# The low halves of W_in, made by GpSimd and VectorE instead of TensorE

## Chip, core and metric

The kernel runs on one core of a Trainium2 chip. The metric is the device time of one execution in microseconds (us). The reference computes in fp32; the kernel keeps each fp32 operand as two fp16 numbers, a high and a low half, and multiplies with three fp16 products.

## What is computed

Causal attention with a decay (4 sequences of 576 tokens, 8 heads of 64), then two MLPs on the 2304 tokens of width 512:

```python
scores = scale * q @ k.T + cum[:, :, :, None] - cum[:, :, None, :]   # causal
x = softmax(scores) @ v                      # 2304 x 512
h = x @ w_in                                 # 512 x 2048
x2 = (h * np.tanh(softplus(h))) @ w_out      # 2048 x 512
h2 = x2 @ w2_in                              # 512 x 1024
solu = h2 * softmax(h2)
out = layer_norm(solu, g_ln) @ w2_out        # 1024 x 512
```

## The kernel before

Three stages overlap. Attention goes over the sequences b and over query tiles i of 128 tokens, in slots of 4, 2 or 1 heads: scores (L436 to L439) into PSUM, a maximum nm on VectorE (L478), the exponential p on ScalarE (L480), a rounding of p and a difference ph (L519, on GpSimd, as fp16 high and low), a transposing DMA pT on SyncE's queue (L524), and the product pv (L550 to L552). A tile ends with x (L565), its split xh (the low half on GpSimd, L569) and a transposing DMA xT, which is the input of the first MLP.

The first MLP works on blocks of 256 tokens. `up` (L787) makes 128 columns of h with 12 matmuls, four chunks of the contraction by three products; `mish` turns h into the pair gt on ScalarE, VectorE and GpSimd (its low half at L814); `down` (L831) adds the second layer. Of block 0 it walks through the 16 column groups n = 0 to 15 while the weights are still being prepared. The second MLP (Stage2) starts when attention is done.

The weights W_in and W_out come as 64-bit numbers, in 16 loads of 1 MB (8 slots each, `Weight.load`, L121, two buffers). `conv` rebuilds fp32 with three VectorE instructions (L134, L136, L138) and then forms a gram matrix with eight matmuls (L157) for a bound. Two slots make a group: `bound` turns the gram into a power-of-two scale, `high` rounds the scaled slot to fp16 on ScalarE (L199), and `low` makes the low half on TensorE, for each of the two 512-column parts of a slot a product of the fp32 weights with a scaled diagonal (L206, seen in the trace as two fp32 passes) and a product of the high half with the identity (L207), whose sum in PSUM ScalarE writes out (L208). Group g of W_in serves n = 4g to 4g+3 of `up`. In the SBUF tile win or wout the fp32 numbers of a slot lie where the next slot's halves will be, so a slot's high half is written after the previous slot's low half has been read.

These steps lie in a list, `wsteps`, in the order of the slots, W_in's pair, then W_out's pair; a step is a load, a conversion, a high or a low. The attention slots ahead of block 0 take WS0 steps each, the half-steps of the main loop WS1 each, and `up` and `down` pull further steps when theirs are missing. A scheduler then reorders each engine's instructions by its own timeline; on the chip each engine runs its list in order, waiting where a semaphore tells it to, and so does SyncE with its DMA issues. Names in the trace: wi_r and wo_r are the loaded numbers, wi_b and wo_b the bounds, wi_d and wo_d the diagonals, sp the PSUM banks that scores and low halves share.

Of the kernel before, what the change touches and what calls it, by code (L numbers as in the profile page):

```python
# [24 lines left out]
NF1 = DFF // P  # L25
# [10 lines left out]
PTB = 2  # L36
R0 = 9
GRP = [4, 2, 1, 1, 1]
WS0 = 4
WS1 = 5  # L40
WPF = 2
S2P = 1
EB = 190
DL = 2
A0 = 16
XB = 3
S2A = 10
# [30 lines left out]
def part_of(w, n):  # L78

    fr, c = divmod(2 * n, w.shape[0] // P)  # L80
    return w[c * P:(c + 2) * P, fr * 512:(fr + 1) * 512].rearrange("(s p) e -> p s e", p=P)
# [143 lines left out]
def emit(tc, q, k, v, f, w_in, w_out, w2_in, w2_out, g_ln, out):  # L225
# [6 lines left out]
    ident = const.tile([P, P], BF16, name="ident")  # L232
# [321 lines left out]
    def fin(b, i):  # L554
# [41 lines left out]
    W1 = Weight(  # L596
        tc, wst, "wi", win, NC1 * DFF // 512, lambda n: part_of(w_in, n), across, group=4,
        after=lambda: pend.get("pt"), gram=grams)
# [13 lines left out]
    def w1_split(n):  # L612
        g, r = divmod(n, W1.group)
        if r == 0:
            W1.bound(g)
            nc.vector.tensor_copy(wps[g], W1.p(g))
        W1.high(n, ident)

    def w2_split(n):
        g, r = divmod(n, W2.group)  # L620
# [1 line left out]
            W2.bound(g)  # L622
            nc.vector.tensor_tensor(rho[:, g:g + 1], wps[g], W2.p(g), op=ALU.mult)
        W2.high(n, ident)

    def w1_low(n):
        W1.low(n, ident, bank)

    def w2_low(n):
        W2.low(n, ident, bank)  # L630
# [43 lines left out]
    def slot_mid():  # L674
        n = pos["k"] - 1
        if 0 <= n < len(seq):
            step_h(*seq[n])
# [26 lines left out]
    wsteps, wdone = [], set()  # L704
    order = [(w, 2 * g + n) for g in range(4) for w in (W1, W2) for n in range(2)]
    for x in range(len(order) + WPF):
        if WPF <= x < len(order):
            wsteps.append((order[x][0].load, order[x][1]))
        if x >= WPF:
            w, n = order[x - WPF]  # L710
            wsteps.append((w.conv, n))
            if n % 2:
                for m in (n - 1, n):
                    wsteps += [(x, m) for x in ((w1_split, w1_low) if w is W1 else (w2_split, w2_low))]
    wsteps.append((w2_final, 0))

    def wgo(n):
        for _ in range(n):
            if wsteps:
                f, a = wsteps.pop(0)  # L720
                f(a)
                wdone.add((f, a))
# [32 lines left out]
    for n in range(n0 + LAG):  # L755
        slot()
        if n:
            wgo(WS0)
    raw0.close()
# [132 lines left out]
    def att_slots(n):  # L892
# [5 lines left out]
        if j == 0:  # L898
            lo = max(lo, n0 + LAG + min(need[1] - n0, (r + 1) * (need[1] - n0) // A0))
        hi = need[j + XB] - 1 if j + XB < NBLK else len(seq) + LAG  # L900
# [7 lines left out]
    for hn in range(2 * (NF + 5)):  # L908
        n, half = divmod(hn, 2)
# [4 lines left out]
        if half == 0:  # L914
            if n % 2 == 0 and 0 <= n // 2 - 1 < NF // 2:
                mish_b(n // 2 - 1)
            if att_now:
                slot_mid()
            if live:
                while n < NF1 and (w1_low, n // 4 * 2 + 1) not in wdone:  # L920
                    wgo(1)
                up(n)
        else:
            if live and n % 2:
                while n > NF1 and wsteps:
                    wgo(1)
                mish_a(n // 2)
            if n % 2 == 0 and 0 <= n // 2 - 1 < NF // 2:
                mish_c(n // 2 - 1)
            if att_now:  # L930
                slot_mid()
            tgt = n - 2 if (n > DL + 8 or n >= NF) else n - DL
            while done["d"] < min(tgt, NF):
                if done["d"] // 2 not in gts:
                    break
                while done["d"] < NF1 and (w2_low, done["d"] // 2) not in wdone:
                    wgo(1)
                down(done["d"])
                done["d"] += 1
        if att_now:  # L940
            slot_pe()
        wgo(WS1)
        while live and pos["k"] < att_slots(hn):
# [178 lines left out]
```

## Time and profile before

| | us |
|---|---|
| median of 3 runs | 863.57 (863.52 to 867.65) |
| profiled execution | 868.76 |
| its span | 867.0 |
| TensorE busy | 766.6 |
| VectorE, ScalarE, GpSimd busy | 594.2, 563.7, 394.2 |

The span is the time from the first to the last instruction of one execution that the hardware profiler recorded. An engine's busy time is the sum of its instructions' durations; matmuls are pipelined, so a busy TensorE need not be at its peak. A view of waits names who waited for whom; the chain of waits follows back, from the last instruction, what released each step.

### The profile page before, as it was taken

Reading aid. Unit: us, or ns where it says so; the run is one execution under the profiler, and the core shown is the slowest. Engines: PE = TensorE matmul, PEld = TensorE weight load, DVE = VectorE, ACT = ScalarE, POOL = GpSimd, SP = SyncE. Lnnn points to the kernel's source line nnn. Section 1 sums busy time; section 2 is a strip of 40 time slices with the busy share of each in tenths; the row PEclk is TensorE's granted clock in tenths of the full one; section 3 lists DMA queues with packets and bytes.
Section 4 is the critical chain, followed back from the end, with each engine's and each line's share of the span. In section 5 each row is a group of like instructions: output and inputs, shape, how many; then the busy total and the mean of one; then the engine's idle time right before and its main releaser. Section 6 shows DMA issues by size and latency. Waiting matters only on the chain.

```text
span 867.0 us, 16642 instructions
## 1 busy us (share of the span) xinstructions
PE 766.6 (88%) x6255; PEld 481.0 (55%) x6255; DVE 594.2 (69%) x1160; ACT 563.7 (65%) x1234; POOL 394.2 (45%) x321
## 2 busy tenths in 40 slices
PE   0468998779999997998889899987999999999998
PEld 0335565557667665676556667654555554444443
DVE  6797954668867898669887654689656454666451
ACT  5648687868878877787876666776965544333331
POOL 2232333447876565765678653226733132012110
PEclk9979999969999999999999999998999999999999
DMA  9998544487799968998797542751022424344443
GB/s 242 228 268 251 175 122 80 87 163 144 151 197 172 163 131 149 169 181 148 164 165 121 113 80 56 191 210 61 26 37 61 97 50 73 86 109 99 107 87 85
DMA packets 328573, 114.90 MB, mean 133 GB/s; under 512 B 317676, under 2 KB 317676, under 8 KB 328492
## 3 DMA queue, kind: packets, MB, share of 16 engines
q1 hardware_dynamic: 328492, 113.84, 63.7%
q8 instruction: 49, 0.80, 0.4%
q14 instruction: 32, 0.26, 0.1%
HBM read 46.59 MB, written 9.55 MB: 65 GB/s over the span
## 4 chain that ended last, share of the span: by engine, by line
PE 40%; DVE 19%; DMA 16%; ACT 9%; issue 9%; POOL 6%; SPq 1%; DVEq 0%; POOLq 0%; ACTq 0%
PE h L1030 10%; PE o L1070 10%; PE x L831 7%; PE h L787 7%; DMA pT<-ph 5%; POOL ph L519 3%; DMA wo_r<-in_moe_w_out_dram 2%; DVE ta L804 2%; POOL gt L814 2%; ACT p L480 2%; DMA xT<-xh 1%; DMA w2i_r<-in_moe_w_in_dram 1%; DVE th L808 1%; DVE vt L215 1%; DVE ph L516 1%
## 5 line engine op out<-in xcount | busy, mean ns | idle before, releaser
L831 PE MATMUL x<-wout,gt 128*128 128x512 f16 x864 | 218.4, 386 | 17.0 <-DVE x2h L860 8.4
L787 PE MATMUL h<-xT,win 128*128 128x256 f16 x1728 | 221.0, 279 | 1.8 <-DMA xT<-xh 1.8
L519 POOL TENSOR_TENSOR ph<-p,ph 128x512 f16<-128x512 f32 (+4 forms) x120 | 155.4, 1301 | 92.0 <-ACT ph L518 42.3
L787 PEld LDWEIGHTS <-win 128*128 128x128 f16 x1728 | 170.0, 100 | 45.1 <-issue 5.5
L814 POOL TENSOR_TENSOR gt<-th,gt 128x512 f16<-128x512 f32 x72 | 92.5, 1286 | 128.7 <-ACT gt L813 122.0
L831 PEld LDWEIGHTS <-gt 128*128 128x128 f16 x864 | 80.5, 99 | 96.4 <-issue 12.5
L1058 POOL TENSOR_TENSOR z<-sl,z 128x1024 f16<-128x1024 f32 x18 | 38.7, 2150 | 138.2 <-DVE s2c L1037 111.3
L1030 PE MATMUL h<-w,x2T 128*128 128x512 f16 x432 | 98.0, 379 | 0.9 <-POOL w L222 0.9
L1070 PE MATMUL o<-wo,zT 128*128 128x512 f16 x432 | 96.5, 379 | 0.5 <-DMA zT<-z 0.5
L550 PE MATMUL pv<-vt,pT 128*128 128x64 f16 (+3 forms) x480 | 68.6, 200 | 23.3 <-DMA pT<-ph 22.9
L808 DVE SCALAR_TENSOR_TENSOR th<-ta,th 128x512 f32<-128x512 f32 x72 | 64.6, 898 | 30.5 <-ACT ta L807 28.0
L436 PE MATMUL sp<-kt,qa 128*128 128x128 f16 (+3 forms) x480 | 68.7, 219 | 15.6 <-ACT p L480 9.6
L480 ACT ACTIVATE p<-sp,nm 64x64 f32<-64x64 f32 (+7 forms) x128 | 61.2, 484 | 27.3 <-DVE nm L478 12.9
L813 ACT CAST gt<-th 128x512 f16<-128x512 f32 x72 | 44.4, 616 | 44.2 <-DVE th L808 42.7
L437 PE MATMUL sp<-kt,qb 67*128 67x128 f16 (+3 forms) x480 | 70.5, 219 | 2.5 <-DMA kt<-dd 2.5
L1030 PEld LDWEIGHTS <-x2T 128*128 128x128 f16 x432 | 42.3, 98 | 51.4 <-issue 1.2
L1070 PEld LDWEIGHTS <-zT 128*128 128x128 f16 x432 | 42.2, 98 | 51.5 <-DMA zT<-z 0.9
L804 DVE TENSOR_SCALAR ta<-ta 128x512 f32<-128x512 f32 x72 | 53.7, 746 | 23.5 <-ACT ta L799 23.2
L550 PEld LDWEIGHTS <-pT 128*128 128x128 f16 (+3 forms) x480 | 44.3, 100 | 45.8 <-DMA pT<-ph 29.6
L552 PE MATMUL pv<-vt,pT 128*128 128x64 f16 (+3 forms) x480 | 67.8, 195 | 0.0
L551 PE MATMUL pv<-vt,pT 128*128 128x64 f16 (+3 forms) x480 | 67.8, 195 | 0.0
L805 ACT ACTIVATE ta<-ta 128x512 f32<-128x512 f32 x72 | 45.3, 631 | 34.0 <-DVE ta L804 33.8
(231 smaller groups left out, 1462.6 us busy)
## 6 DMA issues: line engine op xcount, KB each, us to landing
wi_r<-in_moe_w_in_dram SPq DMA_DIRECT2D x8, 1024.0 KB
wo_r<-in_moe_w_out_dram SPq DMA_DIRECT2D x8, 1024.0 KB
rawk<-in_k_dram SPq DMA_DIRECT2D x25, 256.0 KB
rawv<-in_v_dram SPq DMA_DIRECT2D x25, 256.0 KB
x2d<-x2h SPq DMA_DIRECT2D x18, 256.0 KB
out_dram<-ro SPq DMA_DIRECT2D x18, 256.0 KB
w2i_r<-in_moe_w_in_dram SPq DMA_DIRECT2D x4, 1024.0 KB
w2o_r<-in_moe_w_out_dram SPq DMA_DIRECT2D x4, 1024.0 KB
```

Source lines behind the costliest of these rows:

```text
L436: nc.tensor.matmul(o, qa[:, h, r0:r1_], kc[:, h, a0:a1], start=True, stop=False)
L437: nc.tensor.matmul(o, qb_[:67, h, r0:r1_], kc[:67, H + h, a0:a1], start=False, stop=(c != i))
L480: nc.scalar.activation(pv[:m, g * (i + 1) * P + off:g * (i + 1) * P + end], s3[:, g, off:end], AF.Exp, bias=nm[:m, g:g + 1], accum_out=rs[ ...
L519: nc.gpsimd.tensor_tensor(p4[:, :, 1], pv3, p4[:, :, 0], op=ALU.subtract)
L550: nc.tensor.matmul(o, pT[a0:a1, k, :m], vh, start=(c == 0), stop=False)
L787: nc.tensor.matmul(ph, win[:, (fi // 4) * NC1 + c, col:col + P], x[:, lx * NC1 + c, :], start=(m == 0), stop=(m == 3 * NC1 - 1))
L804: nc.vector.tensor_scalar(ta, ta, E20, 1.0, op0=ALU.min, op1=ALU.add)
L808: nc.vector.scalar_tensor_tensor(th, ta, 2.5, th, op0=ALU.subtract, op1=ALU.mult)
L814: nc.gpsimd.tensor_tensor(gt[:, 1], th, gt[:, 0], op=ALU.subtract)
L831: nc.tensor.matmul(o, gt[:, lg, n % 2, t * P:(t + 1) * P], wout[:, fi, lw * 512:(lw + 1) * 512], start=(first and m == 0), stop=(last and ...
L1030: nc.tensor.matmul(h[:, half * 512:(half + 1) * 512], x[:, lx * NC1 + c, :], self.w2[:, half * NC1 + c, lw * 512:(lw + 1) * 512], start=(n ...
L1070: nc.tensor.matmul(o, zT[:, lz * NF2 + c, :], self.wo[:, c, lw * 512:(lw + 1) * 512], start=(n == 0), stop=(n == 3 * NF2 - 1))
```

## The change

For W_in the pair `high` and `low` is replaced by `split`, a function that the kernel already uses elsewhere; W_out keeps TensorE. A string W1P says, slot by slot, which form: slots 0 and 1 take the form 0 (ScalarE rounds, VectorE makes the difference), slots 2 to 7 the form 1 (ScalarE scales the fp32 numbers in place, GpSimd rounds them and makes the difference). With a step less for each slot of W_in, WS0 goes from 4 to 3 and WS1 from 5 to 4, so the steps of both weights are spread over the slots differently. The changed kernel's lines are numbered one higher up to the functions, and two lower behind them.

```diff
-WS0 = 4
-WS1 = 5
+WS0 = 3
+WS1 = 4
+W1P = "00111111"
...
     def w1_split(n):
...
-        W1.high(n, ident)
+        W1.split(n, on_pool=int(W1P[n % len(W1P)]))
...
-    def w1_low(n):
-        W1.low(n, ident, bank)
...
-                    wsteps += [(x, m) for x in ((w1_split, w1_low) if w is W1 else (w2_split, w2_low))]
+                    wsteps += [(x, m) for x in ((w1_split,) if w is W1 else (w2_split, w2_low))]
...
-                while n < NF1 and (w1_low, n // 4 * 2 + 1) not in wdone:
+                while n < NF1 and (w1_split, n // 4 * 2 + 1) not in wdone:
```

```python
def split(nc, hi, lo, x, scale, on_pool):
    if on_pool == 0:
        nc.scalar.activation(hi, x, AF.Copy, scale=scale)
        nc.vector.scalar_tensor_tensor(lo, x, scale, hi, op0=ALU.mult, op1=ALU.subtract)
        return
    nc.scalar.activation(x, x, AF.Copy, scale=scale)
    if on_pool == 1:
        nc.gpsimd.tensor_scalar(hi, x, 1.0, 0.0, op0=ALU.mult, op1=ALU.add)
...
    nc.gpsimd.tensor_tensor(lo, x, hi, op=ALU.subtract)
```

TensorE's order just ahead of the first L787, before (win is W_in's tile; the eight gram products and then L787 follow):

```order
L352 MATMUL sum<-wo_b,ones 128x1
L206 MATMUL sp_148<-win,wi_d_567 128x512
L207 LDWEIGHTS ident
L207 MATMUL sp_148<-win,ident 128x512
L206 MATMUL sp_146<-win,wi_d_567 128x512
L207 LDWEIGHTS ident
L207 MATMUL sp_146<-win,ident 128x512
L157 LDWEIGHTS win
L157 MATMUL gram<-win 128x128
```

The same place now (eight gram products of wout and then the first layer, now L785, follow):

```order
L553 MATMUL pv_1_502<-vt_1_289,pT_1_6_541 128x64
L158 LDWEIGHTS win
L158 MATMUL gram<-win 128x128
...
L207 MATMUL sp_148<-wout,wo_d_473 128x512
L207 MATMUL sp_146<-wout,wo_d_473 128x512
L208 LDWEIGHTS ident
L208 MATMUL sp_148<-wout,ident 128x512
L208 LDWEIGHTS ident
L208 MATMUL sp_146<-wout,ident 128x512
L353 LDWEIGHTS ones
L353 MATMUL sum<-wi_b,ones 128x1
```

W_in's products are gone, and of W_out one slot's stand here, behind the second tile's last pv.

VectorE's order around the maximum of the second tile's last two heads (nm_1_6, rows 75 to 85 of its list), before:

```order
L136 SCALAR_TENSOR_TENSOR win<-wi_r_361,win 128x1024
L172 TENSOR_REDUCE wo_b<-gram 128x1
L478 TENSOR_REDUCE nm_1_4_503<-sp_146 128x2
L138 SCALAR_TENSOR_TENSOR win<-wi_r_361,win 128x1024
L174 TENSOR_SCALAR wo_b<-sum 128x1
L94 TENSOR_SCALAR wo_b<-wo_b 128x1
L96 TENSOR_SCALAR wo_b<-wo_b 128x1
L134 TENSOR_SCALAR win<-wi_r_407 128x1024
L176 RECIPROCAL wo_b<-wo_b 128x1
L623 TENSOR_TENSOR rho<-wpt,wo_b 128x1
L478 TENSOR_REDUCE nm_1_6_570<-sp_146 128x2
```

Now (rows 70 to 79; L216 is the new difference of W_in, L135 to L139 are the conversions):

```order
L566 TENSOR_TENSOR x_0_0_458<-pv_0_371,rr_0_455 128x512
L139 SCALAR_TENSOR_TENSOR wout<-wo_r_303,wout 128x1024
L216 SCALAR_TENSOR_TENSOR win<-win,wi_b 128x2x512
L135 TENSOR_SCALAR win<-wi_r_349 128x1024
L569 CAST xh_0_460<-x_0_0_458 128x512
L426 COPY qb_126<-qa_2_437 64x1024
L479 TENSOR_REDUCE nm_1_6_534<-sp_147 128x2
L173 TENSOR_REDUCE wo_b<-gram 128x1
L137 SCALAR_TENSOR_TENSOR win<-wi_r_349,win 128x1024
L216 SCALAR_TENSOR_TENSOR win<-win,wi_b 128x2x512
```

The maximum stands ahead of most of that conversion and of the next one's start, and behind one difference; that of heads 4 and 5 has moved up to row 45.

GpSimd's order around the last group of W_in (rows 48 to 57 of its list), now; in the kernel before no instruction of win stands on GpSimd:

```order
L520 TENSOR_TENSOR ph_2_6_939<-p_1_129,ph_2_6_939 128x3x128
L520 TENSOR_TENSOR ph_3_0_1070<-p_0_128,ph_3_0_1070 128x4x128
L220 TENSOR_SCALAR win<-win 128x2x512
L570 TENSOR_TENSOR xh_2_1178<-x_0_2_1176,xh_2_1178 128x512
L223 TENSOR_TENSOR win<-win 128x2x512
L520 TENSOR_TENSOR ph_3_0_1070<-p_1_129,ph_3_0_1070 128x4x128
L220 TENSOR_SCALAR win<-win 128x2x512
L812 TENSOR_TENSOR gt_1680<-th_1652,gt_1680 128x512
L223 TENSOR_TENSOR win<-win 128x2x512
L812 TENSOR_TENSOR gt_1733<-th_1704,gt_1733 128x512
```

The four instructions of the group stand between xh, ph and gt; those of the two groups before it stand in a row, with one xh and one ph among the first of the last.

## Rows read from the trace of the kernel before

**Rows 1.** The page's head: busy us (share) xinstructions by engine.

```profile
span 867.0 us, 16642 instructions
PE 766.6 (88%) x6255; PEld 481.0 (55%) x6255; DVE 594.2 (69%) x1160; ACT 563.7 (65%) x1234; POOL 394.2 (45%) x321
```

**Rows 2.** Busy time by stretch: stretch, length, engines, clock, DMA share, GB/s.

```profile
36.00:78.00 42.00, 28.29 (x207) 16.00 (x207) 38.20 (x76) 27.25 (x57) 15.06 (x11) 0.88 1.00 254
78.00:156.00 78.00, 71.73 (x530) 45.36 (x529) 47.55 (x99) 60.64 (x116) 25.06 (x17) 0.98 0.51 136
156.00:190.00 34.00, 23.17 (x282) 17.70 (x281) 24.69 (x60) 24.34 (x61) 17.12 (x14) 0.76 0.70 131
190.00:867.00 677.00, 636.02 (x5182) 395.96 (x5179) 458.34 (x883) 431.37 (x954) 327.66 (x264) 0.98 0.61 119
```

**Rows 3.** Chain of waits, 45 to 140 us: start us, us, what.

```profile
61.32 3.44 PE sp L206 x4
...
68.95 0.03 PE pv L550
...
77.81 2.23 PE h L787 x19
...
80.99 0.47 PE gram L157 x8
...
129.68 4.79 POOL ph L519
...
134.49 3.71 DMA pT<-ph
```

**Rows 4.** Timeline of VectorE, 38 to 140 us: start, us, instruction.

```profile
52.71 0.67 DVE L478 TENSOR_REDUCE nm<-sp 128x2 f32<-128x512 f32 x1
...
57.04 0.68 DVE L478 TENSOR_REDUCE nm<-sp 128x2 f32<-128x512 f32 x1
```

**Rows 5.** Timeline of SyncE's queue, 0 to 160 us.

```profile
61.87 1.23 SPq L524 DMA_TRANSPOSE pT<-ph  x1
```

**Rows 6.** Timeline of TensorE, 16 to 160 us.

```profile
70.55 1.07 PE L206 MATMUL sp<-win,wi_d 128*128 128x512 f32 x2
...
71.67 1.02 PE L206 MATMUL sp<-win,wi_d 128*128 128x512 f32 x2
...
124.33 2.78 PE L787 MATMUL h<-xT,win 128*128 128x256 f16 x24
```

**Rows 7.** Groups by line, 0 to 160 us: busy, mean ns | idle before.

```profile
L206 PE MATMUL sp<-win,wi_d 128*128 128x512 f32 x32 | 18.3, 671 | 2.9 <-DVE wi_d L197 1.8 <-ACT win L208 1.1
...
L208 ACT ACTIVATE win<-sp 128x512 f16<-128x512 f32 x16 | 9.1, 592 | 4.6 <-PE sp L352 2.7 <-PE sp L207 1.9
```

**Rows 8.** Tile w, Stage2's split: ns min/median/max, first and last start.

```profile
L217 ACT ACTIVATE w<-w,w2i_b x4: 1132/1133/1134, 588.0 to 591.1; 128x1024 f32<-128x1024 f32 x4
L219 POOL TENSOR_SCALAR w<-w x4: 1046/1156/1495, 589.2 to 606.8; 128x1024 f16<-128x1024 f32 x4
L222 POOL TENSOR_TENSOR w<-w x4: 2129/2578/3100, 590.4 to 608.1; 128x1024 f16<-128x1024 f32 x4
```

**Rows 9.** Tile vt (attention's v): VectorE's difference.

```profile
L215 DVE SCALAR_TENSOR_TENSOR vt<-rawv,scv,vt x14: 734/750/1697, 44.0 to 445.7; 128x512 f16<-128x512 f32 x10, 64x512 f16<-64x512 f32 x4
```

**Rows 10.** Timeline of GpSimd, 30 to 200 us.

```profile
111.44 0.92 POOL L519 TENSOR_TENSOR ph<-p,ph 128x384 f16<-128x384 f32 x1 [8.17 <-issue]
...
128.35 6.11 POOL L519 TENSOR_TENSOR ph<-p,ph 128x384 f16<-128x384 f32 x2
```

**Rows 11.** Timeline of VectorE beside the last of these.

```profile
129.80 1.21 DVE L138 SCALAR_TENSOR_TENSOR wout<-wo_r,wout 128x1024 int32<-128x1024 int32 x1
...
132.47 1.21 DVE L138 SCALAR_TENSOR_TENSOR wout<-wo_r,wout 128x1024 int32<-128x1024 int32 x1
```

**Rows 12.** Waits of SyncE's queue, 0 to 200 us: us, times, longest.

```profile
SPq L524 <- POOL gt L814: 31.3, 2, 22.5
```

**Rows 13.** Waits of TensorE, 78 to 190 us.

```profile
PE pv L550 <- DMA pT<-ph: 9.1, 6, 2.2
```

## Prediction

> **What bounds the kernel now.** I read the page's head first: TensorE is busy for 766.6 of 867.0 us and the next engine, VectorE, for 594.2 [rows 1]. Then the busy time by stretch, since the change touches only the first 156 us [rows 2]. From 36 to 78 us VectorE is busy for 38.2 of 42 and TensorE for 28.3: the weight conversions, the preparation of the first attention rows and the scores all pass through VectorE, so it is the first limit there. From 78 us (the first matmul of the MLP's first layer, L787) to 156 us TensorE is busy for 71.7 of 78, with VectorE at 47.6 and GpSimd at 25.1: TensorE is the bound. From 156 to 190 us TensorE falls to 23.2 of 34 at a granted clock of 0.76 (part of the stretch at 1.2 GHz); it waits for the transposes of the probabilities, 9.1 us in 78 to 190 [rows 13]. From 190 us on it is busy for 636 of 677. So an early saving should reach the end, if no wait replaces it.
>
> Third, the chain of waits ahead of the first L787 [rows 3]: four fp32 passes of L206 for W_out (two low halves, 3.44 us), the attention product pv at 68.95, then VectorE, GpSimd and a transposing DMA, and L787 at 77.81. Low halves on TensorE stand on this chain.
>
> **What the change removes.** Each of the 8 slots of W_in has two low halves, each an fp32 product with the scaled diagonal (L206) and a product with the identity (L207). The trace counts fp32 passes: 32 rows are 16 products [rows 7]. From the start of one half to the next takes 1.12 us (70.55 to 71.67, [rows 6]), so TensorE loses 16 x 1.12 = 17.9 us. ScalarE loses 16 evacuations, 9.1 us [rows 7]. Its 8 roundings become 8 passes of about the same length (six fp32 scalings at 1.13, [rows 8], two roundings), so its net is -9.1; it has slack in 78 to 156 (60.6 of 78, [rows 2]) and I cost this at nothing.
>
> **What it adds.** Slots 0 and 1: two VectorE differences of 128x1024. The trace has 128x512 at 0.75 median [rows 9], so 1.5 each is my estimate, bounded by 0.75 and the 1.7 that the longest 128x512 took. Slots 2 to 7: on GpSimd a cast and a difference each. Stage 2 does the same operation on the same shape: cast 1.05 to 1.50, difference 2.13 to 3.10, medians 1.16 and 2.58 [rows 8]. That is 19 to 28 us of GpSimd, which has 53 free in 78 to 156. Throughput is no problem; latency and order are.
>
> **Term 1, the first L787 comes earlier: -7.0.** Two parts. First, the maximum (nm) of the last two heads of the second attention tile: the order has it at VectorE's row 85 in the kernel before, behind the next pair of conversions, and at row 76 now, about where heads 4 and 5 stood. These two stand at 52.71 and 57.04 [rows 4], 4.3 apart; one new difference of W_in comes ahead of it, of whose 1.5 I charge half: -3.6. Second, that tile's last transpose is issued at 61.87 [rows 5]; a transpose took 3.71 to land [rows 3], so pv could go at 65.6 and went at 68.95, behind the low halves of W_out. The order now puts these behind pv: -3.4. If only the second part arrives, the term is -3.4; with no charge for the difference it is -7.7; and if the transposes land as late as now, it is nothing.
>
> **Term 2, TensorE's work after the first L787: -5.8.** By the order, 8 low halves of W_in and 4 of W_out stand ahead of the first L787 before, and 0 and 2 now. Behind it were 8 + 12, and are 14: six fewer, 6.7 us. Two more gram groups of eight move behind it, at 0.47 each [rows 3], +0.9. The other 11.2 us of the 17.9 lay ahead of it, where TensorE was not the limit; what they are worth is in term 1.
>
> **Term 3, new waits of TensorE: +8.2.** The first-layer matmuls of columns 4, 8 and 12 (n of the function up) read slots 2 and 3, 4 and 5, 6 and 7. A pair now takes one scaling (1.13, the second is hidden) and two casts and differences in line on GpSimd: 1.13 + 2 x (1.05 + 2.13) = 7.5 us at the fastest rows, 8.6 at the medians, 10.3 at the slowest [rows 8]. Before, TensorE made these halves itself and was not idle. What covers the wait is what the order places between the reduction of the group's bound and its first matmul; for the last group 24 first-layer matmuls (2.78, [rows 6]), three fp32 products (a row shows 1.07 each, the overlap taken off 2.6 in all, [rows 6]) and, as my estimate, 1.4 of scores and pv: 6.8 us. So 0.7, 1.8 or 3.5 us stay uncovered per pair; I take the median's 1.8, three times, 5.4. In the last group the order puts xh, ph and gt between the split instructions on GpSimd, three at 0.92 [rows 10]: 2.8. Sum 8.2; ends 0 (the scheduler finds other work) and 3 x 3.5 + 2.8 = 13.3 without holds. Queued behind the splits on GpSimd are ph, whose transpose feeds pv, and the first gt, which feeds the second layer. On SyncE the load of slot 5 stands behind a transpose of such a ph. I price these in the rival below, not here.
>
> **The sum** is -7.0 - 5.8 + 8.2 = -4.6 us. The profiled execution took 868.76 (span 867.0, 1.8 around it), 5.2 above the median of the runs shown, 863.57; its sum would give 864.2. I apply the difference to the median: **859.0**.
>
> **Rival A, everything is covered: 850.8.** TensorE always has other work, term 3 is nothing, -12.8. For it: GpSimd is two thirds idle in 78 to 156 [rows 2]. Against: GpSimd's order is fixed, and a pair's latency alone exceeds the cover I found.
>
> **Rival B, GpSimd is starved by VectorE: 870.7, slower.** Between 128.35 and 134.46 us two GpSimd differences of 128x384 took 6.11 us, while one alone took 0.92 [rows 10]; one of them took 4.79 of the chain [rows 3]. In the same time VectorE ran conversions back to back, among them those at 129.80 and 132.47, each reading two tensors of the chip's memory [rows 11]. A difference held like this costs 4.79 - 0.92 = 3.9 us more. The splits of slots 2 to 5 stand, by the order, among the last conversions. With three such holds on the path the sum is -4.6 + 11.7 = +7.1. It is slower by over 0.5% from 8.9 us of holds on, between two and three. SyncE makes it worse: it already waited 31.3 us in two transposes for GpSimd [rows 12], and loads stand behind them. Against: half of the splits may fall into VectorE's gaps. The Trainium skill's page "SBUF — State Buffer", section "Who interferes with whom", says that VectorE and GpSimd share a pair of ports under an exclusive lock, and that a VectorE instruction with two inputs in SBUF and a GpSimd instruction that reads SBUF block each other for a whole instruction. By that rule every split that meets a conversion is held, and this rival would be the forecast; the 6.11 us agrees with it, the stage-2 rows of 2.13 show that it need not happen.
>
> **Rival C, the start does not move: 866.0.** The 16 DMA engines are full in 36 to 78 us (share 1.00, [rows 2]); if transposes and loads set the first L787, term 1 is nothing, and -5.8 + 8.2 = +2.4, within 0.5%. For it: the loads of the weights keep their pace. Against: from 61.32 on the chain runs through L206, pv and what follows it, not through a load of weights [rows 3].
>
> **How the numbers follow.** The bound for a difference is 0.5%, 4.3 us, about what a measurement of this kernel can tell from no change. Forecast 0.40 (855 to 863, of it 0.24 below 859.25 and 0.16 within), A 0.20, B 0.23 (0.21 slower, 0.02 within), C 0.15, and 0.02 for something slower that I don't name. Faster 0.44, same 0.33, slower 0.23. The whole program is scheduled anew behind the weights, with 41 us of TensorE's idle time in 190 to 867 to move; I allow 2 us either way for it. The range reaches from a little below A to B: 849.0 to 871.0.
>
> **What would show it.** Right: L206 with 32 rows instead of 64; the first L787 near 70 to 71 us; pv of the second tile ahead of L206; TensorE's idle time ahead of L787 put down to GpSimd's win differences, some 5 to 8 us in all; ScalarE's busy time 9 us down, GpSimd's 19 to 28 up. A: no wait of L787 on GpSimd. B: single GpSimd differences of win over 4 us beside VectorE's conversions, the last W_out load later than now relative to the first L787, the second block's first L787 not earlier than now. C: the first L787 still near 77. The prediction is wrong in its base if the stretch behind 156 us, where the transposes set the pace, swallows or adds more than 3 us by itself.

## Result and profile after

The changed kernel took **870.32 us** in the median (865.47 to 874.85, 17 runs), the kernel before 865.10 in the same comparison (861.74 to 871.09, 17 runs). The ratio is 1.0057 with a 95% interval of 1.0035 to 1.0079: slower by 5.2 us. The forecast was 4.6 us faster. The two profiled executions that are compared below lie closer together, 871.24 and 868.76, since that of the kernel before is 3.7 above its median. The time lies inside the forecast's range, beside the number of its rival B.

The page's head for the kernel after, to be laid beside [rows 1] (engine, busy us, share, instructions):

```profile
span 869.4 us, 16537 instructions
PE 755.3 (87%) x6207; PEld 477.1 (55%) x6207; DVE 599.9 (69%) x1158; ACT 555.0 (64%) x1218; POOL 419.7 (48%) x333
```

The work did move: TensorE is busy for 11.3 us less, ScalarE for 8.7 less, GpSimd for 25.5 more, VectorE for 5.7 more. But 17.9 us were taken off TensorE and only 11.3 are gone, and its idle time (span less busy) rose from 100.4 to 114.1. So the span's +2.4 is -17.9 of work removed (the forecast's 1.12 for each of 16 low halves), +6.6 of the same work done more slowly, and +13.7 of idle time. The table of stretches says where, beside [rows 2] (stretch, length, busy us of TensorE, its weight loads, VectorE, ScalarE, GpSimd, then granted clock, DMA share, GB/s):

```profile
36.00:78.00 42.00, 20.20 (x174) 14.39 (x174) 32.75 (x66) 23.13 (x50) 20.59 (x11) 1.00 0.92 239
78.00:156.00 78.00, 60.08 (x442) 37.73 (x439) 60.44 (x98) 48.90 (x91) 41.65 (x28) 0.85 0.52 141
156.00:190.00 34.00, 25.50 (x311) 17.78 (x308) 23.73 (x50) 25.67 (x62) 15.61 (x13) 0.94 0.49 96
190.00:867.00 677.00, 639.73 (x5214) 399.15 (x5211) 457.03 (x901) 437.11 (x968) 332.58 (x266) 0.98 0.61 121
```

From 78 to 156 us TensorE was idle for 6.3 us and is now idle for 17.9, and its granted clock there fell from 0.98 to 0.85: part of that stretch runs at 1.2 in place of 2.4 GHz, behind the new gaps. From 89 to 92 us, behind the idle 4.7 us ahead of L158 below, the granted clock is 0.50, and a pass of L207 takes 1.06 us there, 0.59 at 95.6. VectorE's busy time rose by 12.9 us in this stretch, though it has one instruction less there (98, before 99).

The price of the clock can be read from work that the change left alone, W_out's 32 fp32 passes, ahead of 200 us. The first line is of before (L206), the second of after (L207, the same code; busy us, mean ns | idle before):

```profile
L206 PE MATMUL sp<-wout,wo_d 128*128 128x512 f32 x32 | 17.6, 655 | 1.6 <-ACT wout L208 1.6
...
L207 PE MATMUL sp<-wout,wo_d 128*128 128x512 f32 x32 | 22.3, 820 | 5.0 <-DVE wo_d L198 2.7 <-DVE ipwo L635 2.3
```

These passes alone take 4.7 us more, most of the 6.6.

What TensorE waits for in 78 to 190 us is not what I forecast. Its waits in the kernel after (engine, line, waited for: us, times, longest), beside [rows 13]:

```profile
PE pv L551 <- DMA pT<-ph: 9.2, 5, 4.0
PE gram L158 <- DVE win L139: 4.7, 1, 4.7
PE sp L207 <- DVE wo_d L198: 2.5, 1, 2.5
PE sp L207 <- DVE ipwo L635: 2.3, 1, 2.3
PE gram L158 <- DVE wo_b L178: 2.3, 1, 2.3
```

The wait for the transposes is as long as before (9.2 against 9.1). New are four longer waits for VectorE, of 2.3 us and more: a conversion (L139), the diagonal wo_d, the bounds (the longest for VectorE before was 1.2). No wait of L785 is put to a low half made by GpSimd.

The chain of waits of after, 45 to 140 us, shows how these come about (start us, us, what), beside [rows 3]:

```profile
48.98 8.16 POOL qn L223
57.15 3.18 DMA qa<-qn
...
73.00 7.03 DMA wi_r<-in_moe_w_in_dram
...
86.42 1.95 DVE win L139
88.42 1.04 PE gram L158 x8
...
120.79 2.98 POOL win L223
123.85 1.98 POOL win L220
125.90 2.44 POOL win L223
128.34 10.03 issue
138.40 0.93 POOL ph L520
139.34 3.69 DMA pT<-ph
```

It now runs over GpSimd's qn, the load of W_in's slot 4 that starts at 73.00 (before, slots 4 and 5 were loaded from 64.93 on), conversions on VectorE, and GpSimd's split of slots 4 and 5. The load is late by way of qn: VectorE's list has the copy qb ahead of a conversion, qb waits for qa, which is transposed from qn, and starts at 60.35; the loads that need the converted buffers come behind.

The timelines of GpSimd and VectorE, read side by side, show that the two hold each other. First GpSimd (start us, us, instruction):

```profile
48.98 8.14 POOL L223 TENSOR_TENSOR qn<-rawq,qn 128x512 f16<-128x512 f32 x1 [2.77 <-ACT qn L222]
57.08 1.60 POOL L520 TENSOR_TENSOR ph<-p,ph 128x512 f16<-128x512 f32 x1
...
79.16 2.12 POOL L223 TENSOR_TENSOR win<-win 128x1024 f16<-128x1024 f32 x1
...
120.79 2.97 POOL L223 TENSOR_TENSOR win<-win 128x1024 f16<-128x1024 f32 x1
123.85 1.97 POOL L220 TENSOR_SCALAR win<-win 128x1024 f16<-128x1024 f32 x1
125.90 2.44 POOL L223 TENSOR_TENSOR win<-win 128x1024 f16<-128x1024 f32 x1
```

Then VectorE at the same times:

```profile
49.07 1.27 DVE L216 SCALAR_TENSOR_TENSOR win<-win,wi_b 128x1024 f16<-128x1024 f32 x1
...
52.34 1.21 DVE L137 SCALAR_TENSOR_TENSOR win<-wi_r,win 128x1024 int32<-128x1024 int32 x1
53.47 1.27 DVE L216 SCALAR_TENSOR_TENSOR win<-win,wi_b 128x1024 f16<-128x1024 f32 x1
54.80 1.21 DVE L139 SCALAR_TENSOR_TENSOR win<-wi_r,win 128x1024 int32<-128x1024 int32 x1
...
119.84 1.94 DVE L137 SCALAR_TENSOR_TENSOR win<-wi_r,win 128x1024 int32<-128x1024 int32 x1
...
121.78 2.00 DVE L624 TENSOR_TENSOR rho<-wpt,wo_b 128x1 f32<-128x1 f32 x1
...
126.29 2.13 DVE L198 TENSOR_SCALAR wo_d<-ident,wo_b 128x128 f32<-128x128 bf16 x1
```

The same instructions in before:

```profile
49.62 1.22 POOL L222 TENSOR_TENSOR qn<-rawq,qn 128x512 f16<-128x512 f32 x1 [2.68 <-ACT qn L221]
...
80.09 0.13 DVE L623 TENSOR_TENSOR rho<-wpt,wo_b 128x1 f32<-128x1 f32 x1
...
81.03 0.28 DVE L197 TENSOR_SCALAR wo_d<-ident,wo_b 128x128 f32<-128x128 bf16 x1
```

From 48.98 to 57.12 the difference of qn takes 8.14 us, where it took 1.22 at 49.62 in before, and VectorE's instructions beside it, the two new differences of W_in (L216) among them, have their ordinary lengths, up to the one that starts at 56.41: GpSimd is held. At 121.78 it is the other way about: rho, one column, takes 2.00 us (0.13 to 0.14 in before) until a GpSimd difference ends at 123.76; wo_d takes 2.13 at 126.29 (0.28 to 0.29 in before from 78 us on). The Trainium skill's page "SBUF — State Buffer", section "Who interferes with whom", says that the one that comes first keeps the shared ports for a whole instruction; the rows of 121.78 and 126.29 agree, and qn, held for 8.14 us over several VectorE instructions, goes further than that.

To count this I compared each VectorE instruction from 78 to 156 us with its undisturbed length (for the same instruction and shape, the length that a tenth of its rows in all profiled kernels do not exceed) and added what was over: 6.1 us before, 18.6 after. The texts below call this sum VectorE's excess.

A second count: matmuls started by a given time, W_in's low products not counted. By 78 us it is 242 before and 253 after, with the first L785 at 72.90 (before 77.81); by 156 us it is 746 and 691. Told as time, against the same matmul of before: the 242nd starts 2.1 us earlier in after, the 300th 4.9 us later, the 700th (146 us in before) 12.2 later, the 746th 4.9 later, and the last 2.4 later. So the early gain is gone within a few us of 78.

### The profile page after: what moved, and what is told of

It reads as the page before. It is cut to its first block, busy times and chain, and to the rows that moved or that the text cites. A ratio compares the mean times of both kernels' runs of the same rounds, so it can differ in the third digit from the quotient of the medians.

```text
span 869.4 us, 16537 instructions
## 1 busy us (share of the span) xinstructions
PE 755.3 (87%) x6207; PEld 477.1 (55%) x6207; DVE 599.9 (69%) x1158; ACT 555.0 (64%) x1218; POOL 419.7 (48%) x333
## 4 chain that ended last, share of the span: by engine, by line
PE 36%; DVE 19%; DMA 14%; ACT 10%; issue 10%; POOL 9%; SPq 2%; DVEq 0%; ACTq 0%; POOLq 0%
PE h L1028 10%; PE o L1068 10%; PE h L785 6%; PE x L829 6%; DMA pT<-ph 4%; POOL ph L520 3%; DVE th L806 2%; DVE ta L802 2%; DMA kt<-kn 2%; ACT p L481 2%; DMA w2i_r<-in_moe_w_in_dram 2%; POOL gt L812 1%; DMA qa<-qn 1%; PE sp L207 1%; POOL ph L515 1%
## 5 line engine op out<-in xcount | busy, mean ns | idle before, releaser
L785 PE MATMUL h<-xT,win 128*128 128x256 f16 x1728 | 220.0, 277 | 1.8 <-DMA xT<-xh 1.0
L520 POOL TENSOR_TENSOR ph<-p,ph 128x512 f16<-128x512 f32 (+4 forms) x120 | 152.5, 1277 | 95.7 <-ACT ph L519 48.8
L785 PEld LDWEIGHTS <-win 128*128 128x128 f16 x1728 | 169.5, 100 | 45.8 <-issue 7.4
L551 PE MATMUL pv<-vt,pT 128*128 128x64 f16 (+3 forms) x480 | 70.6, 202 | 36.1 <-DMA pT<-ph 30.9
L806 DVE SCALAR_TENSOR_TENSOR th<-ta,th 128x512 f32<-128x512 f32 x72 | 67.4, 938 | 24.2 <-ACT ta L805 22.4
L437 PE MATMUL sp<-kt,qa 128*128 128x128 f16 (+3 forms) x480 | 69.6, 220 | 10.8 <-ACT p L496 3.7
L552 PE MATMUL pv<-vt,pT 128*128 128x64 f16 (+3 forms) x480 | 69.6, 197 | 1.0 <-DVE vt L216 1.0
L553 PE MATMUL pv<-vt,pT 128*128 128x64 f16 (+3 forms) x480 | 69.5, 197 | 0.0
L479 DVE TENSOR_REDUCE nm<-sp 128x1 f32<-128x320 f32 (+7 forms) x88 | 48.5, 558 | 28.8 <-PE sp L440 17.6
```

Source lines behind the costliest of these rows:

```text
L437: nc.tensor.matmul(o, qa[:, h, r0:r1_], kc[:, h, a0:a1], start=True, stop=False)
L520: nc.gpsimd.tensor_tensor(p4[:, :, 1], pv3, p4[:, :, 0], op=ALU.subtract)
L551: nc.tensor.matmul(o, pT[a0:a1, k, :m], vh, start=(c == 0), stop=False)
L785: nc.tensor.matmul(ph, win[:, (fi // 4) * NC1 + c, col:col + P], x[:, lx * NC1 + c, :], start=(m == 0), stop=(m == 3 * NC1 - 1))
L806: nc.vector.scalar_tensor_tensor(th, ta, 2.5, th, op0=ALU.subtract, op1=ALU.mult)
```

## Experiments

All medians in us; the kernel before took 864.4 to 865.9 in the groups of runs with which these were compared. The interval is that of the ratio to before.

| run | what | us | 95% of the ratio |
|---|---|---|---|
| e1_split_pace45 | after, pace 4/5 | 873.0 | 1.0052 to 1.0099 |
| e2_split_all_vector | after, all slots on VectorE | 873.6 | 1.0059 to 1.0120 |
| e3_tensor_pace34 | before, pace 3/4 | 872.9 | 1.0050 to 1.0113 |
| e4_no_low_halves | after, no low halves | 855.8 | 0.9864 to 0.9913 |
| e5_no_low_pace45 | e4, pace 4/5 | 858.2 | 0.9889 to 0.9941 |
| e6_only_vector_slots | after, slots 0, 1 only | 862.5 | 0.9942 to 0.9982 |
| e7_only_gpsimd_slots | after, slots 2 to 7 only | 873.4 | 1.0050 to 1.0110 |
| e8_hybrid_pace45 | slots 0 to 3 TensorE, 4 to 7 GpSimd | 870.2 | 1.0031 to 1.0072 |
| e9_gpsimd_fill_only | e7, fills for GpSimd's splits | 861.3 | 0.9904 to 0.9959 |
| e10_cast_on_scalar | after, cast on ScalarE | 870.8 | 1.0037 to 1.0074 |
| e11_vector01_tensor | slots 0, 1 VectorE, 2 to 7 TensorE | 876.9 | 1.0095 to 1.0168 |
| e12_tensor_pace56 | before, pace 5/6 | 864.8 | 0.9963 to 0.9994 |
| e13_after_qn_vector | after, qn by VectorE | 865.0 | 0.9961 to 1.0004 |
| e14_before_qn_vector | before, qn by VectorE | 870.2 | 1.0026 to 1.0062 |
| e15_vector_tensor_qn | e11, qn by VectorE | 878.2 | 1.0118 to 1.0169 |
| e16_vector_slots_qn | e6, qn by VectorE | 857.7 | 0.9882 to 0.9936 |
| e17_after_short_conv | after, shorter conversion | 867.2 | 0.9984 to 1.0031 |
| e18_before_short_conv | before, shorter conversion | 856.3 | 0.9842 to 0.9925 |

### The pace, and what the low halves are worth

The change has two parts, the split and the pace (WS0, WS1), and my sum had priced only the first. Four runs and a fifth take them apart. In e4 and e5 ScalarE writes zeros in place of W_in's low halves, so nobody makes them; the rest of the work is whole.

```
e1 (from after):   WS0 = 4, WS1 = 5
e2 (from after):   W1P = "0"        # ScalarE's high half, VectorE's difference
e3 (from before):  WS0 = 3, WS1 = 4
e4 (from after):   W1P = "3"
+    if on_pool == 3:
+        nc.scalar.activation(hi, x, AF.Copy, scale=scale)
+        nc.scalar.activation(lo, x, AF.Copy, scale=0.0)
+        return
e5: e4 with WS0 = 4, WS1 = 5
```

> The changed kernel with the old pace, WS0 = 4 and WS1 = 5. Theory G (the loss comes from GpSimd's splits: their latency, their place in its order and their blocking of VectorE): the time stays within 3 us of the changed kernel, about 5 us (0.6%) above the kernel before. Theory P (the loss comes from the slower pace of the weight steps, loads and conversions later): the loss is gone, at most 1 us above the kernel before, and the wait of the gram products for the conversion of slot 4 (4.7 us at 88 us) disappears. Theory S (block 0 is not bound by TensorE, its saved products are worth nothing there): no statement, about as the changed kernel.

> The changed kernel with all eight slots of W_in in form 0: ScalarE rounds, VectorE makes the difference (six more of 1.27 us on VectorE, 7.6 us), nothing of W_in on GpSimd. Theory G: faster than the kernel before, by 3 to 9 us, since TensorE's saving stays and the waits for GpSimd go. Theory P: about as the changed kernel, 4 to 6 us above the kernel before. Theory S: 0 to 8 us above the kernel before, VectorE being the bound.

> The kernel before (both low halves on TensorE) with the new pace, WS0 = 3 and WS1 = 4. Theory P: 4 to 8 us above the kernel before. Theories G and S: within 3 us of it.

> The changed kernel with W_in's low halves left out: ScalarE rounds the high half and writes zeros as the low half (two passes of about 1.15 us for a slot), nothing of W_in on TensorE, GpSimd or VectorE. It shows what TensorE's 17.9 us are worth when nobody else takes the work. Theory G: 6 to 13 us below the kernel before. Theory P: 0 to 5 us above it. Theory S: within 3 us of the kernel before, or above it.

> The kernel after with W_in's low halves left out (ScalarE writes zeros for them), as in the run without low halves, and the old pace of 4 and 5 weight steps a slot. Theory P (the slower pace itself costs, whoever makes the low halves): the 8.5 us that the kernel before lost at pace 3/4 come back here, so 855.8 - 8.5 = 847 us. Theory I (pace and low halves interact: what a slow pace delays is TensorE's low products, which then fall into a stretch where TensorE is the bound; with no low halves the pace is nearly free): 854 to 858 us. Theory F (a faster pace puts the weights' work of ScalarE and VectorE ahead of the attention's): over 858 us.

Measured, by pace:

| who makes W_in's low halves | pace 4/5 | pace 3/4 |
|---|---|---|
| TensorE | 864.4 (before) | 872.9 |
| GpSimd and VectorE | 873.0 | 870.3 (after) |
| VectorE alone | - | 873.6 |
| nobody | 858.2 | 855.8 |

Three things follow. The slower pace costs 8.5 us where TensorE makes the halves, but it gives 2.4 to 2.7 where it doesn't; so the pace is not why the changed kernel is slower, though I had left it out. (The 2.4 and 2.7 are hardly more than the spread of the runs.) With nobody making them the time falls by 6.3 us at the old pace and 8.6 at the new: that is about the most that a new owner of the work can gain, ScalarE's passes of zeros included. And GpSimd with VectorE takes 14.5 us back (870.3 less 855.8), VectorE alone 17.8.

No theory fits all five runs. Theory G had e1 (2.7 us from after) and e4 (8.6 below before), missed e3, and asked for 3 to 9 us less than before in e2, which took 9.2 more. Theory P had e3, a little beyond its 8 us, and missed e1, e4 and e5; its wait for the conversion grew in e1 (9.4 us from 36 to 200 us, after 6.5). e5 ended at the border of theories I and F.

The stretches of e4 show what TensorE does when nothing takes the place of its low halves:

```profile
78.00:156.00 78.00, 69.33 (x572) 45.37 (x570) 54.07 (x108) 64.50 (x123) 24.36 (x21) 0.95 0.59 151
```

Its idle time is 8.7 us (after 17.9), the clock 0.95 (0.85), with 823 matmuls started by 156 us (691).

### Which slots cost it

```
e6: W1P = "00333333"      e7: W1P = "33111111"      (both with the branch of e4, pace 3/4)
```

> The kernel after at its pace 3/4, with low halves only for slots 0 and 1 (ScalarE and VectorE, as in after); those of slots 2 to 7 are zeros by ScalarE, so that GpSimd has no part of the weights. The 14.5 us between after (870.3) and the run without low halves (855.8) are divided by this run and the next. Theory V (the first two slots cost it: VectorE's differences at 49 and 53 us hold GpSimd's qn for 8.14 us, and pT, the diagonal pv and the start go later): 866 to 870 us. Theory Q (GpSimd's six slots between 78 and 156 us cost it): 855 to 859 us.

> The kernel after at its pace 3/4, with low halves only for slots 2 to 7 (GpSimd's cast and difference, as in after); those of slots 0 and 1 are zeros by ScalarE. Theory V: 856 to 860 us, with qn at about 49 us back near 1.2 us. Theory Q: 866 to 870 us, with TensorE's idle time of 78 to 156 us near the 17.9 us of after.

Slots 0 and 1 alone cost 6.8 us over e4, the six of GpSimd 17.6; together they cost 14.5, so the two prices do not add up. e6 lies between the ranges of the two theories and e7 above that of theory Q: Q took the larger part, and V was not empty either. One line each: GpSimd in e6, where the hold of qn is back although GpSimd has no part of the weights, and the stretch in e7.

```profile
50.80 8.58 POOL L227 TENSOR_TENSOR qn<-rawq,qn 128x512 f16<-128x512 f32 x1 [3.31 <-ACT qn L226]
```

```profile
78.00:156.00 78.00, 62.27 (x504) 41.10 (x503) 56.06 (x98) 53.23 (x105) 39.40 (x27) 0.90 0.53 147
```

In e7 qn took 2.20 us, and TensorE's idle time in the stretch is 15.7 us.

### The hold of qn

One digit moves the differences of qn of the first sequence, five of them, from GpSimd to VectorE, in four kernels; it also saves ScalarE a pass for each.

```
-QKV = "002"
+QKV = "000"
```

> The kernel after with the difference of qn and of its like in block 0 made by VectorE in place of GpSimd (L223), so that nothing of it can be held on GpSimd. Theory N (the price of the slots 0 and 1 on VectorE, 6.7 us, is the hold of qn at 49 us, 8.14 us in place of 1.22, and pT and the diagonal pv behind it): 863 to 866 us. If that hold is without a price, as the count of matmuls done by 78 us says (249 in after, 250 in before, W_in's low products not counted): 868 to 873 us, since VectorE gets three differences more.

> The control: the kernel before with the same move of qn's differences to VectorE. qn took 1.22 us there, so theory N has nothing to take away: 864 to 867 us, the price of three more differences on VectorE. Below 862 us the move is good by itself and the run of after with it says less.

> The run with low halves on the slots 0 and 1 alone (VectorE; W_in's other low halves left out, 862.5 us), with qn's differences on VectorE. Theory N: 855 to 858 us, as without any low halves (855.8). If VectorE's two differences cost it themselves: 861 to 865 us.

> The version with slots 0 and 1 on VectorE and slots 2 to 7 on TensorE (876.9 us, 11 us slower than before, with qn held for 8.31 us and 20.3 us of TensorE's waits for pT between 36 and 200 us), with qn's differences on VectorE. Theory N: 864 to 869 us. If the two differences of slots 0 and 1 delay VectorE's other work themselves: 873 to 879 us.

In after the move gives 5.3 us (870.3 to 865.0), in e6 4.8 (862.5 to 857.7), and in before, where nothing was held, it costs 4.9 (865.3 to 870.2, 3 us beyond its range). e13 and e16 lie where theory N put them: by these two the hold of qn costs some 5 us, and it ate what the earlier start had brought. The stretch ahead of 78 us in e13 goes with that:

```profile
36.00:78.00 42.00, 23.46 (x199) 16.83 (x199) 34.86 (x72) 22.87 (x47) 11.82 (x9) 1.00 1.11 254
78.00:156.00 78.00, 56.42 (x412) 33.69 (x410) 59.34 (x97) 45.68 (x87) 39.73 (x27) 0.87 0.47 127
```

TensorE is busy for 3.3 us more from 36 to 78 us than in after, with 278 matmuls started by 78 (253; the expectation of e13 has 249 for after and 250 for before, where the traces have 253 and 242). The stretch behind is no better than in after: 21.6 us idle. With the hold gone, a wait of TensorE appears that after did not show (36 to 200 us):

```profile
PE h L785 <- POOL win L220: 5.7, 3, 3.0
```

These are three waits of the first layer for GpSimd's splits, the ones that my third term had asked for. So e13 ends level with before (interval 0.9961 to 1.0004), still 9 us above the kernel without low halves.

e15 goes against the theory: with qn on VectorE it stays at 878.2. What makes the mixture of e11 and e15 (below) so slow is another cause. Three more traces make the price of 5 us doubtful. e1 and e2 have the same VectorE differences in slots 0 and 1, but qn took 2.88 and 2.61 us there, and they are no faster than after (873.0 and 873.6); in e17 (below) it took 1.15, for a gain of 3.2. So the differences do not always bring the hold, and a kernel without it can be as slow.

### GpSimd's six slots

```
e9:  W1P = "33444444"; form 4 is form 3 and then
+            for _ in range(3):
+                nc.gpsimd.memset(lo, 0.0)
e10: W1P = "00222222"     # hi by nc.scalar.copy, the difference on GpSimd
```

> As the run with low halves on GpSimd's six slots alone (873.4 us; W_in's low halves of slots 0 and 1 left out), but GpSimd's cast and difference of slots 2 to 7 are replaced by three fills of the same tile with zeros (about 3 x 1.04 us, the fill of 1024 columns in the profile of before, against 3.4 us), after ScalarE's zeros; W_in's low halves are left out altogether. GpSimd's queue is held as long and TensorE waits for it as late, but nothing is read by GpSimd. Theory L (the price is VectorE held by GpSimd's reads: 23.9 us over undisturbed durations in 36 to 156 us there, 13.3 us without GpSimd's part): VectorE's excess falls back to 9 to 14 us and the time to 856 to 861 us. Theory O (the price is order and latency on GpSimd: ph, gt and xh behind the split, up behind the low half): 869 to 874 us.

> The kernel after with the cast of slots 2 to 7 moved from GpSimd to ScalarE; GpSimd keeps the difference alone, which is the instruction that holds VectorE. GpSimd's part of a slot falls from 3.7 to 2.3 us. Theory L with the difference as the holder: VectorE's excess stays near 20 us, 867 to 871 us. Theory L with both as holders, or theory O: a third to a half of the 14.5 us goes, 863 to 866 us.

e9 took 861.3, just above the range of theory L (856 to 861); 5.5 of the 17.6 us of e7 are left when GpSimd is occupied about as long but reads nothing. e10 took 870.8: over a third of GpSimd's time for the weights goes (the casts are 8.4 of 22.3 us in after), and nothing is gained, though ScalarE has six passes more there; theory L with the difference as the holder had asked for 867 to 871. Nor is it the weights' loads: those of W_in's last slots are issued at 97.61 and 105.86 us in e7 and at 97.67 and 104.88 in e9. So about 12 us go with the splits that GpSimd reads for, not with its being busy. What of it is the reading is not shown: in e9 the high halves come from ScalarE, and nothing of a slot waits for GpSimd's difference of the slot before. And VectorE's excess from 36 to 156 us did not fall as theory L asked: 19.9 in e9, 24.0 in e7, 13.4 in e4. From 78 to 156 us e7 and e9 differ in it by 1 us, and in time by 12, so the excess does not set the time. The fills hold VectorE as well, if other instructions of it. GpSimd in e9, then VectorE beside that fill:

```profile
73.78 3.39 POOL L219 MEMSET win<- 128x1024 f16 x3 [3.61 <-ACT win L216]
```

```profile
73.75 1.52 DVE L135 TENSOR_SCALAR win<-wi_r 128x1024 int32<-128x1024 int32 x1 [0.18 <-DMA wi_r<-in_moe_w_in_dram]
75.31 1.22 DVE L137 SCALAR_TENSOR_TENSOR win<-wi_r,win 128x1024 int32<-128x1024 int32 x1
```

The conversion with one input (L135) takes 1.52 us beside a fill, against 0.68 at 50.27 in after; the one with two inputs (L137) keeps its 1.2. Beside a GpSimd cast and the start of a difference the latter is held too (1.94 at 119.84 in after). The same section of the Trainium skill's page "SBUF — State Buffer" says that an instruction with two inputs does not contend with a GpSimd instruction that only writes; these rows agree.

### Is VectorE's time the bound?

```
e17 (from after), e18 (from before), in Weight.conv:
-            nc.vector.scalar_tensor_tensor(
-                t, w[:, :, :, 1], -0x40000000, t, op0=ALU.bitwise_and, op1=ALU.bitwise_or)
```

> The kernel after with one VectorE instruction less in every conversion of W_in and W_out (L137, the one that puts in the sign and the top bit of the exponent; the weights lose their sign): 16 x 1.2 = 19 us of VectorE's time, most of it between 36 and 130 us, and one partner less for GpSimd's differences to collide with. Theory V (VectorE, full of its own work and held by GpSimd, sets the pace of 78 to 156 us in after): 852 to 859 us, 11 us or more off the 870.3. If it is order and latency on GpSimd that costs: 863 to 868 us.

> The kernel before with the same instruction left out (the weights lose their sign there too). Theory V: TensorE is the bound of 78 to 156 us in before, so the 19 us of VectorE are worth less than half of what they are in after: 859 to 863 us. If the conversions set the pace in both kernels, as the loads that wait for them might make them: 850 to 857 us, and VectorE is the bound in before as well.

Theory V fell, and the other way round from what I expected: 19 us less on VectorE give 3.2 us in after (870.3 to 867.2) and 9.3 in before (865.6 to 856.3). e17 lies in the range of the other theory, order and latency on GpSimd (863 to 868), and e18 in that of conversions that set the pace in both kernels (850 to 857). The first line is of e17, the second of e18:

```profile
78.00:156.00 78.00, 68.79 (x561) 45.22 (x560) 48.74 (x95) 59.19 (x113) 36.87 (x27) 0.94 0.59 154
...
78.00:156.00 78.00, 73.59 (x568) 47.19 (x567) 41.01 (x92) 63.98 (x125) 22.79 (x22) 0.98 0.56 128
```

In the stretch itself e17 does what theory V says: TensorE's idle time falls from 17.9 to 9.2 us, with 822 matmuls started by 156 us in place of 691. The end does not follow: TensorE's busy time over the whole span is 761.1 us in e17 against 755.3 in after, for the same 6207 matmuls, at a mean granted clock of 0.963 against 0.968, and of the 131 matmuls that it is ahead of after by 156 us, 83 are left by 250 (1655, 1572). So what is gained in the stretch is in part given back behind it. VectorE's excess is as large as in after (23.0 us in 36 to 156), though some 6 us of it have moved ahead of 78; the hold of qn is gone (1.15 us at 48.04).

In e18 the last two loads of W_in start at 81.4 and 88.3 us (before 93.4 and 95.0), with 290 matmuls started by 78 us (242) and 832 by 156 (746). So VectorE's conversions, with the loads that wait for them, set the pace of before as well, from 78 us on too, where the prediction had TensorE alone.

### Versions that might have beaten both

```
e8:  W1T = 4: slots below W1T by W1.high and W1.low (TensorE), the others by W1.split on GpSimd; WS0 = 4, WS1 = 5
e11: W1T = 2: slots below W1T by W1.split on VectorE, the others by W1.high and W1.low; WS0 = 4, WS1 = 5
e12 (from before): WS0 = 5, WS1 = 6
```

> A version that might beat both: W_in's slots 0 to 3 by TensorE as in before, at a time when TensorE still has idle time (20.2 of 42 us busy in 36 to 78 us in after), slots 4 to 7 by GpSimd as in after, at the old pace 4/5. If the work on TensorE early is free and GpSimd's late splits are covered: the 9 us of TensorE's late products are saved, 856 to 860 us. If each of GpSimd's splits holds back the attention's ph behind it as it does in after (theory Q, about 14.5 us for six slots, so some 10 for four): 864 to 868 us, no gain over before.

> A version that might beat both: W_in's slots 0 and 1 as in after (ScalarE and VectorE), slots 2 to 7 by TensorE as in before, pace 4/5, no part for GpSimd. At the pace 4/5 TensorE's low halves cost 864.5 - 858.2 = 6.3 us, and the two slots on VectorE cost 862.5 - 855.8 = 6.7 us at 3/4. If the earlier start counts (first h matmul near 72 us in place of 77.8): 861 to 863 us; if VectorE's two differences cost as much as the products they replace: 864 to 867 us.

> The kernel before at the pace 5/6. At 3/4 it took 872.9 us, at 4/5 864.5 us. If the loss at 3/4 is TensorE's low products coming late, into the stretch where TensorE is the bound, then they come earlier still and the time is 858 to 863 us; if at 4/5 they already lie in idle time, and more steps a slot only put them ahead of the attention's work: 864 to 870 us.

None is worth having. e8, with four GpSimd slots, took 870.2, more than either of its ranges. e11 lies above both of its own. e12 is within 0.2% of before (by the second of its two readings, 864 to 870): past 4/5 the pace gives nothing. e11 is the slowest but for e15, and I cannot say why: its first matmul of the first layer comes at 80.03 (72.90 in after), and the chain of e15 runs from one load of weights to the next conversion and back:

```profile
75.73 1.24 DVE win L138
...
78.24 7.87 DMA wo_r<-in_moe_w_out_dram
86.14 0.70 DVE wout L136
86.86 2.06 DVE wout L138
```

That the loads come late there is seen; why they do was not tried.

## Why the prediction was wrong

**The step that failed.** In the sum, the start (term 1) counted as a gain of 7.0 us that reaches the end, and the new owners (term 3) cost only what TensorE waits for GpSimd, 8.2 us; what the new differences do to the instructions beside them was put at nothing in it. By the runs, taking the work off TensorE gave 8.7 us (864.5 to 855.8, e4, with the pace) where terms 1 and 2 had 12.8, and the new owners cost 14.5 (855.8 to 870.3) where term 3 had 8.2.

**What the change removes** held: 32 passes in place of 64, ScalarE 8.7 us down (forecast 9.1), GpSimd 25.5 us up (19 to 28; the splits of W_in alone are 22.3).

**Term 2 (-5.8)** held in size: with nobody making the low halves the kernel at the old pace is 6.3 us faster (e5), and there the start did not move (78.39 us), so this is not term 1.

**Term 1 (-7.0)** failed. Its first part, -3.6, came to nothing. The maximum of the second tile's last two heads did come 5.5 us earlier than in [rows 4], but the ph of heads 4 and 5 and of these two stood behind qn on GpSimd until 57.08 and 59.75, and the tile's last transpose was issued at 62.09, where [rows 5] has 61.87. Its second part came nearly whole: the pv behind that transpose starts at 65.87 us, 2.9 earlier than in before (68.78); the other 2.0 of the start were gained between this and L785. In after, on VectorE, SyncE's queue and TensorE:

```profile
51.54 0.68 DVE L479 TENSOR_REDUCE nm<-sp 128x2 f32<-128x512 f32 x1
...
62.09 1.24 SPq L525 DMA_TRANSPOSE pT<-ph  x1
...
72.90 2.67 PE L785 MATMUL h<-xT,win 128*128 128x256 f16 x23
```

And the 4.9 us that the first L785 gained did not reach the end: by 78 us they were worth 11 matmuls, and then TensorE waited 4.7 us for the conversion of slot 4, loaded at 73.00 in place of 64.93. Over the runs the start says nothing of the end: 71.41 with 872.9 us (e3), 78.39 with 858.2 (e5), 87.62 with 864.8 (e12). I had priced the two new VectorE differences at the time that they take from VectorE (half of 1.5), and not at what they do to a GpSimd instruction beside them. That this is worth the 5.3 us of e13 is argued and not shown, since e1 is as slow without the hold.

**Term 3 (+8.2)** was too small, and in after something else stood in its place. Three waits of the first layer for GpSimd's splits at 1.8 us each, 5.4, were its core; after has none, since TensorE is late there already for VectorE, and e13, with qn's hold gone, has three of 5.7 us together. Order and latency without GpSimd's reads cost 5.5 us (e9). So these waits were sized about right. Missing was the rest of the 14.5 us that the work put on GpSimd and VectorE costs: 5.3 go when qn is moved (e13), and 9.2 are left; taking the casts off GpSimd gives nothing (e10). That the rest is what GpSimd's differences and VectorE do to each other is the likely reading and is not shown.

**The pace** was missing from the sum. It is worth -2.4 here (e5 to e4), by luck small; in before it would have been +8.5 (e3 against before).

**Put together by the runs**: 864.5 for before, -6.3 for TensorE's halves, -2.4 for the pace, +14.5 for the new owners is 870.3. This closes because each term is the step from one median to the next; the text above says what of the last is understood.

**Rival B** had the sign and, by its number, the time (870.7), but only part of the cause; that the number fits is luck. I had three GpSimd differences of W_in held by VectorE for 3.9 us each. Those took 2.12 to 2.97 us, about as in [rows 8]; the one held was qn, an attention step that the change did not touch, and from 78 us on it was VectorE that lost time, 12.5 us more than before. Two of its signs were right: the second block did not start earlier (192.72 us, before 186.26), and the last load of W_out came 52.0 us behind the first L785 (before 41.3). The third, a difference of win over 4 us, was not. **Rival A** (everything covered, 850.8) was out of reach: even with nobody making the low halves the time is 855.8 (e4) or 858.2 (e5). **Rival C** (the start doesn't move) was wrong as put, since the start did move, and its 866.0 is off by 4.3.

**The base** held by its own sign, if narrowly: behind 156 us the lag goes from 4.9 to 2.4 us, under the 3 us that the prediction named, with up to 10.8 between. That TensorE alone is the bound from 78 us on did not hold (e18).

**What stays open.** That GpSimd and VectorE hold each other is seen in the rows; that the six slots' last 9 us are this hold is not shown, since e17 took 19 us off VectorE and got 3.2 back, and e7 and e9 lose about the same on VectorE from 78 to 156 us and lie 12 us apart. The three runs of e11, e14 and e15 move 5 to 13 us by edits that should have cost little, so a part of every difference here may be the new order that each edit gives to all that comes behind it, and the clock that goes with TensorE's gaps. A run that gives GpSimd the same reads with nobody waiting for them was not tried.

## What to carry to other kernels

Before work is moved from a full engine to idle ones, measure the kernel with that work left out: here this bound was 6 to 9 us, and every new owner cost that much or more. An engine's idle share says nothing of what it costs its neighbour: look for the two-input VectorE instructions and the GpSimd differences that will run side by side, and count the untouched GpSimd instructions near them too. A first matmul that comes earlier is no gain by itself; count the matmuls started by a later time.

## What was new of the hardware

A GpSimd difference of 128x512 beside a dense row of VectorE instructions took 8.14, 8.58, 8.00 and 8.31 us (after, e6, e10, e11), against 1.15 to 2.9 in the other runs that have it on GpSimd near 50 us: in after thirteen VectorE instructions start beside it before it ends. e1 and e2 have the same new VectorE differences and no such hold (2.88, 2.61), so what decides it is open. In the other direction a VectorE instruction of one column took 2.00 us for 0.14 beside a GpSimd difference. And TensorE's gaps cost twice: for W_out's 32 passes the same work took 22.3 us in place of 17.6, at a granted clock of 0.85 in place of 0.98 in the stretch that holds most of them.
